# Group 0 of the sixth half batch by seven products, its mixed weights in unread quarters of w_in, and another written order

## The chip, the cores and the metric

The kernel runs on one core of one Trainium2 chip. The metric is the device time of one execution in microseconds; a kernel's time is the median of several executions. A profiled execution has a span, from its first to its last instruction, and a time of its own, a little above the span.

## What is computed

Attention over 4 batches, 8 heads, 768 tokens and 64 columns, with a band of 96 keys behind each query and 8 global keys, a bias by distance, and a softmax; then a feed-forward layer with a squared rectifier on the 3072 tokens of 512 columns:

```
scores = scale * q @ k.T + bias;  scores = where(is_global | is_local, scores, -1e9)
attn_out = softmax(scores) @ v
x = attn_out as [3072, 512]
h = maximum(x @ w_in, 0)          # w_in:  512 x 2048
out = (h * h) @ w_out             # w_out: 2048 x 512
```

The input is float32 and the kernel computes in fp16 with float32 sums.

## The kernel before

A half batch (hb 0 to 7) is 384 tokens. For each one the kernel loads q, k and v, turns q and k, forms scores, exponentials and their product with v (`score`, `attend`), turns the result into `xt` (512 columns on partitions, 384 tokens), and applies layer 1 (`w_in`) and layer 2 (`w_out`). Layer 1 of a half batch is 16 tiles of 128 hidden units, m = 0 to 15.

Layer 1 can be done in two ways. `layer1` is the plain one: for each m four matmuls of 384 columns into one bank of PSUM, then a rectification into `hr` and, for each pair of tiles, a square into `h2`. `layer1_group` takes the four tiles of a group g (m = 2g, 2g+1 and the same two 8 higher) as a 2 by 2 block product, of the two halves of w_in's rows, the near and far hidden units, and the two halves of the tokens, and computes it with seven products instead of eight (Strassen's scheme in Winograd's form). Each product is four matmuls of 192 columns. Products p1 to p7 go into two or three banks, a running sum is copied out (`keep`, tile `kept`) where it is used again, and added back (`give`). That needs sums of inputs (`x_mix`, made from `xt` by DVE) and sums of weights, four of them: for groups 1 to 3 in `in_mix`, made once at the start (`list_in_mix`); for group 0 in `late_mix` (`list_late_mix`, line 804). `GROUPS` is 1, 2, 3, and `LAYER1` says for each half batch which jobs stand in what order: a letter or digit is one product of a group (h to n is group 0), an s is a plain tile. Half batches 6 and 7 have all four groups by products; 2 to 5 have group 0 (2 also group 1) plain.

The products never read w_in's far hidden units in the first half of the rows directly. That quarter of group 0 is 2 x 256 columns on 128 partitions.

Layer 2 goes by seven products as well, for pairs of 128-token tiles (`layer2_pair`, `mix_tokens`).

Nothing orders itself: every job is first listed, TensorE's as p, loads as l, all the rest as numbers of one list, and then `Plan.run` emits them in the order of the string `ORDER`, word by word. A word is an engine's letter (p TensorE, a ACT, d DVE, s SP, l a load that POOL issues, g POOL) and the number of the job in its list; digits behind a point are the banks of PSUM that a TensorE job takes. So ORDER fixes each engine's queue, and for most jobs also the engine that does it. Each engine works its queue strictly in this order and waits where a need isn't met. The numbers shift where jobs are added to the lists: with the change TensorE has three more jobs, and the rest five more.

The loads l11, l13, l16 and l17 are w_in's quarters by hidden units, the second, first, fourth and third (512 KB each); l0, l4, l9, l12, l14, l15 are v of the first batch, l18 to l23 are k and q of the third half batch, all of 128 KB. Loads go through one queue.

Of the kernel before, what the change touches and what calls it, by code (L numbers as in the profile page):

```python
# [13 lines left out]
P = 128  # L14
# [37 lines left out]
ORDER = """a4 d1 g2 p0.0 a6 s8 d12 a0 s10 d13 l3 l1 a18 l2 d15 d19 a26 d16 d3 l5 a30 d14 a20 a27 d9 l4 a23 d5  # L52
a22 d17 p1.12+31 a21 l0 p5.34 d11 a7 p10.56 l6 a28 p3 a24 l10 a31 d32 l9 a33 p6 d34 p4.7 a39 l7
p11 d37 a29 p9.0 p8.1 a46 l8 p2.23 d43 a40 p19.7 d35 l11 a47 p7 d55 a25 p13.51 d36 l13 a41 d44
p14.4 p12.67 d48 p15 a42 l12 d59 p17 a49 p16.0 p22.2 d45 l14 p24.4 a52 d51 p23.36 a50 d38 p34.50
l16 d58 a53 p21.7 d64 p25.2 a60 l18 p27.1 d65 a57 p20.4 a61 p32.37 d66 a81 d56 p31.2 l15 p29.6 a73
d68 p18.5 p28.4 d72 a74 p26.3 l19 p36.1 d54 a69 p35.2 p30.7 a86 d70 p33.54 d85 a71 d91 p39.16 a67
p40.27 a77 p37.3 d63 l17 a82 d75 a78 d62 p41.5 a92 d79 d76 p38.0 d84 d80 l21 p45.4 d83 d96 a97 l20
p48.1 a101 a98 p44.2 l23 p47.5 a89 d107 p46.7 a112 p42.0 d111 a108 d110 a93 p43.2 d109 p53.1 a87
l22 p52.5 d102 p50.4 p49.7 d120 a113 d100 l27 a90 d105 p59.6 a116 d119 d106 a103 l29 p55.3 p51.1  # L60
d94 a122 l28 d128 a88 p65.2 d95 a104 a117 d114 p64.5 d99 a118 d146 d191 p58.4 a129 l30 a136 d115
l24 p60.0 a137 d205 l25 p54.3 p62.6 p57.1 a133 p56.7 d125 d121 p63.5 p67.6 a123 d134 d135 a130
d206 p61.1 p72.3 a126 d132 p69.7 d189 a124 p77.5 a131 d156 p70.0 a142 p82.1 d157 d165 a159 p71.4
a160 p74.7 d162 l34 a166 d201 a163 p83.6 d147 a161 l26 p73.0 d164 a167 d158 d148 a138 p84.3 l31
a168 d186 a169 p79.42 d202 l35 a139 d127 p89.01 p81.7 d151 a198 l33 p85 a187 d170 a178 d207 p86
d184 a174 a199 d149 p78.06 a179 l32 p80.45 p88.71 d180 p87 a195 d200 l36 a175 p76.2 d203 a185 d155
p75.7 l37 d193 a196 p91.0 a188 d143 l38 s194 d197 p66.1 a181 d172 l39 a171 d152 p95.3 a173 p90.4
d223 p100.2 d153 s224 a209 a176 d236 p92 d204 d177 p103.7 d208 d237 p68.3 a244 a140 d210 s216
p93.6 a211 d240 p94 a182 d150 a144 d219 p96.1 p104 s217 d225 p97 d183 a245 d221 p98.5 d239 s220
p102.3 a218 d238 p111 d214 d228 s226 l44 p106 d222 d243 l43 s229 p109.61 d213 d227 p110.53 d154  # L70
p99 l40@217 a255 d258 s215 p101 a256 d141 l42@217 d145 a251 d272 d190 p113 l45 a252 a234 p114.53
d254 l41@217 d192 p108.61 p105.0 a248 l46 d246 a261 p107 d253 d259 l47 a262 d257 s260 p115.67 a249
s235 p116.52 l48 a264 p118.3 d230 d250 p131.1 a265 d232 a268 p117.6 d263 a293 p122.7 d231 a273
d266 p121.5 a269 d233 d212 a271 p125.1 d280 s328 p124 d284 p127.2 a283 p126 d241 a278 p123.6 d267
a294 d285 p137.1 s329 d281 p119.4 a288 p132 a287 p129.5 a279 d295 p130 p140 d327 a305 p142 a286
d270 p134.6 a291 d274 a311 p128.1 a292 p135 d289 p133.7 a312 p136 d300 p141.4 a314 d303 a302
p143.1 a299 d313 s242 a296 p139 d330 s282 p138 a304 d405 p112 a309 d315 a301 l50@329 d310 s275
p120 a307 d297 a316 l56 a306 p146.36 d308 s290 p147.42 p145.51 a334 d317 l53 p144.7 a337 d322 s298
a335 l51@329 p148.3 d323 a338 a276 l52 p149.4 d325 a331 d443 d336 l49@329 a326 p151.62 a332
p150.05 d318 p152 d324 l54 a342 d333 p159.1 a343 l57 p157.0 d340 a341 p172.5 d344 a345 p153 l55  # L80
a356 d377 a346 p160.3 a354 p169.6 s378 d319 a348 p158.5 d357 p162 p161 d355 p154.2 d320 a359
p166.3 d407 a351 p164.5 p163 d360 p156 d321 a361 d363 s408 p171.1 d365 a372 p165 d347 a364 p167
a366 p181.5 d368 a369 d339 p170 a367 p175 d349 p177 d373 a362 p174.0 d382 p173.4 a386 p178.3 d380
a374 s409 p176 d376 a393 p180 d375 p155.0 a379 d353 a387 p168.1 d383 a384 d391 a394 s247 p179 d410
s277 p183 a370 s358 p182.5 d392 a352 d388 p184 l58@409 a397 d395 a385 p186.32 d389 l65 s381
p188.10 a399 p187.46 d390 a371 p185.5 l62 d398 a419 s396 p189.7 d411 a423 l59@409 a416 d412 p190.4
l63 a415 d414 a420 p191 a424 d413 l73 a417 d426 p192.13 a428 d422 l61 p193.60 a427 d421 p194.72
p196 a432 d418 l60@409 a429 d425 p198.6 a433 p195 d406 l64 a436 d401 a444 p200.1 d496 a437 p199.0
d447 a430 p202.7 d497 p218.2 s448 d445 p207.3 a475 d402 p197.1 d403 a457 s350 p206.0 d404 s446
a451 d441 p211 a442 d438 p210 a455 d435 p204.2 a462 d434 p205.7 a456 d453 p208 p213 d463 p216.0  # L90
d492 p219.2 a464 d499 d498 s507 p228.3 a454 d468 d439 a458 p209 d505 p223 a465 d476 s508 p203.4
# [113 lines left out]
def kernel(  # L205
# [18 lines left out]
    NFT = d_ff // P  # L224
# [1402 lines left out]
```

## Time and profile before

| | |
|---|---|
| median of 3 runs | 200.61 us (200.53 to 202.39) |
| the profiled execution | 200.26 us |
| its span | 198.5 us |
| TensorE's granted clock | 1.00 |
| DMA | 27.52 MB, mean 139 GB/s |

An engine's busy time is the union of its instructions. Ends of matmuls are modelled and overlap the next start, so the distance from one start to the next is what a matmul costs. PE is TensorE's matmuls, PEld its weight loads, DVE the vector engine, ACT the scalar engine, POOL GpSimd, SP the engine that issues stores and turns by DMA. In a row of a group stand line, engine, operation, output and inputs, shapes and count, then the busy time and the mean ns of one, then the idle time ahead of it and who ended it. In a row of time the first number is the start, the second the duration, in us from the span's start.

### The profile page before, as it was taken

The page shows a single profiled execution, that of the slowest core. Times are in us where ns is not written, and L with a number is a line of the kernel's source. Part 1 is how long each engine was busy: PE and PEld are TensorE (multiplying, and loading weights), DVE is VectorE, ACT ScalarE, POOL GpSimd, SP SyncE. Part 2 cuts the span into 40 slices and gives each one's busy share as a digit, 9 for nine tenths or more (in the row PEclk, how much of TensorE's full clock was granted, in tenths as well). Part 3 has the DMA queues.
Part 4 walks back from the last instruction along what each step waited for, and adds up shares of the span by engine and source line. Part 5 has one row for each costly group of instructions (what it writes and reads, how often), then busy time and mean ns, then how long its engine had stood idle before and what let it go on. Part 6 is the DMA issues. An engine that isn't in the chain of part 4 may idle for free.

```text
span 198.5 us, 5961 instructions
## 1 busy us (share of the span) xinstructions
PE 191.0 (96%) x2369; PEld 162.4 (82%) x2369; DVE 179.5 (90%) x469; ACT 159.9 (81%) x337; POOL 66.9 (34%) x82
## 2 busy tenths in 40 slices
PE   7698999999999999999999999999999999999993
PEld 2576898856998687799788988899889999999992
DVE  7689696898999989999999997999999999999971
ACT  6799896899556889989998999989797889589311
POOL 8996564187107800950293039200000000000000
PEclk9999999999999999999999999999999999999999
DMA  5999999999998999999999979994521330210124
GB/s 155 181 149 196 188 181 171 206 198 155 183 189 94 163 196 220 102 139 109 266 118 156 122 177 143 194 198 104 103 81 39 113 76 1 106 56 0 56 106 159
DMA packets 106987, 27.52 MB, mean 139 GB/s; under 512 B 97104, under 2 KB 104016, under 8 KB 106960
## 3 DMA queue, kind: packets, MB, share of 16 engines
q0 software_dynamic: 74944, 13.11, 90.5%
q1 hardware_dynamic: 30816, 13.45, 32.0%
q10 hardware_dynamic: 1200, 0.59, 1.1%
q8 instruction: 18, 0.29, 0.7%
q14 instruction: 9, 0.07, 0.1%
HBM read 27.26 MB, written 6.29 MB: 169 GB/s over the span
## 4 chain that ended last, share of the span: by engine, by line
PE 82%; DMA 10%; POOL 5%; issue 0%; DVE 0%; POOLq 0%
PE yps L1084 34%; PE hps L844 22%; PE hps L717 12%; DMA w_in_sb<-in_moe_w_in_dram 10%; PE sp L610 5%; PE av L671 4%; PE yps L998 4%; POOL w_mix L396 3%; POOL v L396 1%; PE trp L549 1%; POOL sq L396 1%; POOL sk L396 0%; PE av L1400 0%; POOL far L294 0%; DVE y L258 0%
## 5 line engine op out<-in xcount | busy, mean ns | idle before, releaser
L623 ACT ACTIVATE ex<-sp 128x512 f16<-128x512 f32 x66 | 37.6, 661 | 3.9 <-PE sp L610 3.6
L717 PE MATMUL hps<-xt,w_in_sb 128*128 128x384 f16 (+2 forms) x304 | 38.9, 275 | 0.5 <-DMA w_in_sb<-in_moe_w_in_dram 0.5
L1084 PEld LDWEIGHTS <-h 128*128 128x128 f16 x376 | 33.9, 98 | 4.5
L904 DVE TENSOR_TENSOR hr<-hps,kept 128x384 f16<-128x384 f32 x55 | 29.0, 549 | 2.0 <-PE hps L844 2.0
L717 PEld LDWEIGHTS <-w_in_sb 128*128 128x128 f16 x304 | 24.9, 98 | 7.0 <-DMA w_in_sb<-in_moe_w_in_dram 0.9
L256 ACT COPY kept<-hps 128x384 f32<-128x384 f32 x50 | 24.0, 499 | 5.5 <-PE hps L844 5.4
L1084 PEld LDWEIGHTS <-mixed 128*128 128x128 f16 x272 | 25.4, 98 | 2.7
L396 POOL DMA_DIRECT2D sq<-in_q_dram x19 | 17.2, 904 | 29.2 <-DMA q<-sq 21.3
L396 POOL DMA_DIRECT2D sk<-in_k_dram x19 | 17.1, 901 | 23.2 <-DMA q<-sq 21.4
L256 ACT COPY y<-yps 128x256 f32<-128x256 f32 (+2 forms) x38 | 14.8, 405 | 12.0 <-PE yps L1084 9.2
L844 PEld LDWEIGHTS <-in_mix 128*128 128x128 f16 x272 | 23.0, 98 | 1.3
L744 ACT ACTIVATE hr<-hps 128x384 f16<-128x384 f32 (+1 forms) x38 | 20.3, 549 | 4.5 <-PE hps L717 4.4
L844 PE MATMUL hps<-x_mix,in_mix 128*128 128x192 f16 x204 | 23.2, 246 | 0.0
L396 POOL DMA_DIRECT2D v<-in_v_dram x24 | 21.9, 925 | 1.7 <-DMA w_mix<-in_q_dram 1.0
L1084 PE MATMUL yps<-w_mix,h 128*128 128x256 f16 (+1 forms) x192 | 22.4, 264 | 0.0
L1084 PE MATMUL yps<-w_mix,mixed 128*128 128x256 f16 (+1 forms) x184 | 22.2, 268 | 0.0
L1084 PE MATMUL yps<-w_out_sb,h 128*128 128x256 f16 (+1 forms) x184 | 22.0, 268 | 0.0
L647 DVE TENSOR_TENSOR phat<-ex,mask 128x1024 f16<-128x1024 f16 (+1 forms) x36 | 20.8, 593 | 0.0
L844 PEld LDWEIGHTS <-w_in_sb 128*128 128x128 f16 x236 | 20.0, 98 | 0.9
L944 ACT ACTIVATE h<-hr 128x768 f16<-128x768 f16 x24 | 20.0, 850 | 0.4
L844 PE MATMUL hps<-xt,w_in_sb 128*128 128x192 f16 x160 | 18.8, 246 | 0.0
L758 ACT ACTIVATE h<-hr 128x768 f16<-128x768 f16 (+1 forms) x21 | 15.4, 756 | 0.2 <-DVE hr L746 0.2
(119 smaller groups left out, 370.9 us busy)
## 6 DMA issues: line engine op xcount, KB each, us to landing
out_dram<-y SPq DMA_DIRECT2D x23, 256.0 KB, 2.3
v<-in_v_dram POOLq DMA_DIRECT2D x24, 128.0 KB, 6.8
sq<-in_q_dram POOLq DMA_DIRECT2D x19, 128.0 KB, 6.4
sk<-in_k_dram POOLq DMA_DIRECT2D x19, 128.0 KB, 6.2
w_in_sb<-in_moe_w_in_dram POOLq DMA_DIRECT2D x4, 512.0 KB, 11.1
w_out_sb<-in_moe_w_out_dram POOLq DMA_DIRECT2D x4, 512.0 KB, 12.0
y<-in_k_dram ACTq DMA_DIRECT2D x2, 256.0 KB, 5.0
y<-in_q_dram SPq DMA_DIRECT2D x2, 256.0 KB, 4.4
```

The source lines that it names most:

```text
L256: nc.scalar.copy(out=out, in_=in_)
L396: dma = nc.gpsimd.dma_start(out=dst, in_=src[x.b, :, r0 + t * P:r0 + (t + 1) * P, :] .rearrange("h p d -> p h d"))
L610: nc.tensor.matmul(sp[h][:, i, :], lhsT=lhsT, rhs=x.q[rows, r % HT, a, :], start=True, stop=True)
L623: nc.scalar.activation(out=st["ex"][:, h], in_=sp[h], func=AF.Exp, scale=scale)
L647: eng(e).tensor_tensor(out=x.phat[a][:, :, t0:t0 + n], op=ALU.mult, in0=st["ex"][:, :, i0:i0 + 2 * n].rearrange("p e (t b) c -> p e t (b c ...
L717: nc.tensor.matmul(st["ps"][:, i * n:(i + 1) * n], lhsT=w_in_sb[:, kk, m * P:(m + 1) * P], rhs=x.xt[:, kk, c0:c1], start=kk == 0, stop=kk ...
L744: nc.scalar.activation(out=o, in_=i, func=AF.Relu)
L758: nc.scalar.activation(out=h2, in_=hr, func=AF.Square)
L844: nc.tensor.matmul(st[name][:, i * HC:(i + 1) * HC], lhsT=left(i, kk), rhs=right(kk), start=fresh and i == kk == 0, stop=kk == KK - 1, ski ...
L904: eng(e).tensor_tensor(out=hidden(which)[:, :, cols], in0=sums(name), in1=st[kept], op=ALU.add)
L944: nc.scalar.activation(out=h2, in_=hr, func=AF.Square)
L1084: nc.tensor.matmul(st[bank_name][:, 0:n], lhsT=a(m), rhs=b(m)[:, cols], start=fresh and m == 0, stop=m == HK - 1, skip_group_check=not fresh)
```

## The change

Group 0 of half batch 5 (the sixth) is done by seven products. Its four plain jobs go, seven jobs of four short matmuls come, with their copies, adds, rectifications and squares. The mixed weights of group 0 must then be there before the last half batch's staging of q (`y.sq`), which held three of them, is free; they move into the unread quarters of w_in, of groups 3, 2, 1 and 0. Each sum now waits for the plain products that read its quarter, and for the mixed weights of the first loading that are made from it. The weight sums are listed at the sixth half batch instead of the seventh.

```diff
-          4: "AasBbCscDEdefF123ss45gG67", 5: "1A2BCDs3E45sF6abcdefgGs7s",
+          4: "AasBbCscDEdefF123ss45gG67", 5: "1A2BCDh3E45iF6jabckdlefgGm7n",
...
-        if any(m in (NFT // 2, NFT // 2 + 1) for m in ms):
-            plain_jobs.append(job)
+        for g in {m % (NFT // 2) // 2 for m in ms if m >= NFT // 2}:
+            plain_jobs[g].append(job)
...
-    plain_jobs = []
+    plain_jobs = [[] for _ in range(4)]
...
     def list_late_mix():
-        y = halves[NHB - 1]
         near, far = slice(0, 2 * P), slice(d_ff // 2, d_ff // 2 + 2 * P)
         w = [[w_in_sb[:, a * KK:(a + 1) * KK, ms] for a in range(2)] for ms in (near, far)]
+        places = (GROUPS[2], GROUPS[1], GROUPS[0], 0)
+        late_mix.extend(w_in_sb[:, 0:KK, far.start + g * 2 * P:far.stop + g * 2 * P] for g in places)
         for i, a, b in ((0, w[1][0], w[1][1]), (1, 0, w[0][0]), (2, w[0][0], w[1][0]),
                         (3, w[0][1], 1)):
             def late_sum(e, i=i, a=a, b=b):
-                if not late_mix:
-                    rows = y.sq.rearrange("p t h d -> p (t h d)")
-                    late_mix.extend([rows[:, n * KK * 2 * P:(n + 1) * KK * 2 * P].rearrange(
-                        "p (k m) -> p k m", k=KK) for n in range(3)] + [w[1][0]])
...
-            needs = [late_mix_ops[t][0] for t in (a, b) if type(t) is int] + y.turned
-            if i == 3:
-                needs = needs + plain_jobs + late_mix_ops[2]
+            needs = [late_mix_ops[t][0] for t in (a, b) if type(t) is int] + plain_jobs[places[i]]
+            needs = needs + (late_mix_ops[0] + late_mix_ops[2] if i == 3 else
+                             in_mix_ops[0] + in_mix_ops[2])
```

ORDER is another one from its third word on. The loads around w_in, and the words around the new jobs (old ORDER first; in the new one p248, p254, p258, p262, p264, p271 and p273 are the seven products, d538 to d541 the weight sums, a550, a568, a572, d561, d574, d590, d575, d591, a594, a576 and d595 their copies, adds, rectifications and squares):

```
l3 l1 l2 l5 l4 l0 l6 l10 l9 l7 l8 l11 l13 l12 l14 l16 l18 l15 l19 l17 l21 l20 l23 l22
l1 l2 l3 l5 l4 l9 l0 l8 l7 l10 l6 l11 l13 l12 l14 l16 l17 l15 l20 l23 l22 l18 l19 l21
```
```diff
+p109.30 p99 a255 d213 d214 l40@217 a251 d258 s215 p101 d538 a256 l42@217 a252 d257 p114.56 a241
...
+d577 a559 p258.2 p269 d579 p254.3 a544 a568 s601 p262 d541 p274 d593 a572 d580 a586 d561 p271 a560
+p264 d603 p275 s578 a604 d574 a587 d590 p279 d609 a581 d575 s556 p273 d596 a620 d602 p280 a594
+a576 d591 p276.05 d595 p278.13 p277.27 a610 d624 p281.6 a617 d625 a613 p282.0 a622 d628 a611 d626
```

TensorE's jobs around the first readers of w_in's fourth quarter (p49, p51, p59) and its third (p60 and p56), in the old and the new order (the numbers are the same in both up to 247):

```
old: p53 p52 p50 p49 p59 p55 p51 p65 p64 p58 p60
new: p59 p51 p53 p49 p50 p56
```

p49, p59, p58, p60, p64 and p65 are pairs of plain tiles (eight matmuls of 256 columns), p51 and p56 four tiles (sixteen matmuls of 128 columns), p50, p52, p53 and p55 pairs of transposes.

More of the change, by code (lines that the diff above doesn't have):

```diff
@@ L50 @@
 KEEP = [0, 1, 2, 1, 6, 4, 3]
[L52 to L68, printed above, removed]
@@ L99 @@
-a535 p252 d559 a562 p253 a565 p266.4 d527 a580 p260.1 p261 d534 a581 s450 p250.5 p244 d578 a553
-a568 d548 p257 s579 a586 p259.7 d563 p264 a542 p242.4 d551 a567 s560 d554 a552 d574 p269 p263.5
-d566 a583 p248.6 d555 a540 d597 p265 a556 s596 p262 d576 p271 a546 d569 a564 p272 d598 d575 a599
-d572 p254.7 a577 d570 p276 s573 d591 a557 d571 a584 p278.3 d558 s549 d611 d600 p273.26 d635
-p274.15 d633 p275.74 a601 p277 d615 a608 a619 d616 p279.2 a609 d618 a604 p283 a602 d634 d613 a605
-p281.74 d617 s614 a631 p280.16 s593 p282.05 a624 d603 p288 a620 d587 a628 d610 p300.7 s594 p286
@@ new lines @@
+a109 l21 d100 a88 d95 p51.4 d110 a128 d112 p53.0 p49.5 d117 a113 p50.7 d191 p56.3 a116 l28 d105
+p62.2 l27 d104 d129 p52.4 l29 p57.7 d120 d119 p55.6 p60.0 d94 a122 l30 d99 a114 d125 p64.4 a118
+l24 d115 p54.6 d136 a101 p65.5 l25 d130 a123 p58.7 l26 a133 d121 d102 p69.1 d137 p61.4 p71.3 d124
+a156 p63.0 d134 p72.2 a157 d135 p70.6 d189 a132 p67.0 a138 l31 a159 d126 p76.1 a165 l34 d131 a166
+p83.4 d162 d160 a142 d201 p82.5 a158 d167 d163 p74.7 d187 a186 l36 d202 a139 p84.2 d205 a164 d169
+p89.60 d161 a127 d147 p88.34 p79.57 a198 d151 p85 a178 l35 d149 a199 p86 a195 d148 a179 p80.65
@@ L123 @@
+p379 s814 p372 d811 d810 s812 p381 a803 p382 d815 s804 s816 a817 a818"""
 class Op:
```

104 lines of the change are left out of this document (58 added, 46 removed).

## The prediction

> **What bounds the kernel now.** I read the page first, then who waited for whom on TensorE, then the busy time by stretches, then the order of time where a term needs it.
>
> ```profile
> span 198.5 us, 5961 instructions
> ...
> PE 191.0 (96%) x2369; PEld 162.4 (82%) x2369; DVE 179.5 (90%) x469; ACT 159.9 (81%) x337; POOL 66.9 (34%) x82
> ...
> PE   7698999999999999999999999999999999999993
> ...
> DVE  7689696898999989999999997999999999999971
> ACT  6799896899556889989998999989797889589311
> ```
>
> TensorE is idle only in the opening (the first four slices) and in the last slice; DVE is nearly full as well. The view of waits has for PE:
>
> ```profile
> PE sp L1350 <- ACT q L256: 0.9, 1, 0.9
> ...
> PE hps L717 <- DMA w_in_sb<-in_moe_w_in_dram: 0.5, 2, 0.3
> ```
>
> Its only wait behind 20 us is for w_in. So time is TensorE's stream from about 20 us on: work taken from it counts in full, and so does each wait that a new order brings. The stretch of the sixth half batch (hb 5, some 28 us) with the two engines that empty PSUM:
>
> ```profile
> sum 28.00, PE 28.00 PEld 24.77 DVE 27.34 ACT 25.07 POOL 1.10; mean PE 4.00 PEld 3.54 DVE 3.91 ACT 3.58 POOL 0.16
> ```
>
> The sum is over seven stretches from 124 to 152 us. PE has no gap in it, DVE 0.66 us, ACT 2.93.
>
> **The products.** Group 0 of hb 5 is now 4 plain jobs, each of 4 matmuls of 384 columns; it becomes 7 products, each of 4 matmuls of 192.
>
> ```profile
> 127.81 0.81 PE L717 MATMUL hps<-xt,w_in_sb 128*128 128x384 f16 x4
> 128.46 0.49 PE L844 MATMUL hps<-x_mix,in_mix 128*128 128x192 f16 x4
> 128.79 0.49 PE L844 MATMUL hps<-xt,in_mix 128*128 128x192 f16 x4
> 129.12 0.81 PE L717 MATMUL hps<-xt,w_in_sb 128*128 128x384 f16 x4
> 129.77 0.41 PE L844 MATMUL hps<-xt,w_in_sb 128*128 128x192 f16 x3
> ```
>
> From start to start (ends are modelled and overlap) a plain job takes 128.46 - 127.81 = 0.65 us, a product 0.33. So 7 x 0.33 = 2.31 replaces 4 x 0.65 = 2.60: -0.29 us, all of it on the path.
>
> More matmuls need more weight loads, 28 for 16:
>
> ```profile
> L844 PEld LDWEIGHTS <-in_mix 128*128 128x128 f16 x272 | 23.0, 98 | 1.3
> ```
> ```profile
> 149.93 0.68 PEld L844 LDWEIGHTS <-sq 128*128 128x128 f16 x8
> ```
>
> One lasts 98 ns, longer than the 82 ns (0.33/4) that its matmul holds the stream; but eight take 0.68, so (0.68 - 0.098)/7 = 83 ns apart: they overlap and keep up. The Trainium skill, "TensorE: Matmul & The Clock Gate", section "Back-to-back issue gap", speaks against this change: in a stream of load and matmul pairs it has about 81 ns for 128 columns and 131 for 512, so on a line between, as an estimate, 89 for 192 and 114 for 384, and 28 x 89 - 16 x 114 = +0.67 us for my -0.29. The trace disagrees: 0.65/4 = 163 ns for 384 columns, and that decides.
>
> **What empties PSUM.** Kinds and prices, from the groups between 124 and 148 us, first DVE, then ACT:
>
> ```profile
> L904 DVE TENSOR_TENSOR hr<-hps,kept 128x384 f16<-128x384 f32 x9 | 4.6, 550 | 0.0
> ...
> L946 DVE TENSOR_TENSOR h<-hr 128x768 f16<-128x768 f16 x4 | 2.1, 549 | 0.0
> ...
> L914 DVE TENSOR_SCALAR hr<-hr 128x768 f16<-128x768 f16 x3 | 1.1, 351 | 0.0
> ...
> L804 DVE TENSOR_TENSOR sq<-w_in_sb 128x512 f16<-128x512 f16 x2 | 0.8, 418 | 0.0
> ...
> L760 DVE TENSOR_TENSOR h<-hr 128x768 f16<-128x768 f16 x1 | 0.6, 551 | 0.0
> ...
> L929 DVE TENSOR_SCALAR hr<-hr 128x384 f16<-128x384 f16 x1 | 0.2, 249 | 0.0
> ```
> ```profile
> L623 ACT ACTIVATE ex<-sp 128x512 f16<-128x512 f32 x14 | 7.9, 629 | 0.8 <-PE sp L610 0.8
> L944 ACT ACTIVATE h<-hr 128x768 f16<-128x768 f16 x6 | 5.1, 850 | 0.0
> L256 ACT COPY kept<-hps 128x384 f32<-128x384 f32 x9 | 4.2, 496 | 0.1
> ...
> L744 ACT ACTIVATE hr<-hps 128x384 f16<-128x384 f32 x4 | 1.9, 486 | 0.9 <-PE hps L717 0.8
> L912 ACT ACTIVATE hr<-hps 128x384 f16<-128x384 f32 x3 | 1.6, 527 | 0.0
> ...
> L758 ACT ACTIVATE h<-hr 128x768 f16<-128x768 f16 x1 | 0.9, 856 | 0.0
> ```
>
> Removed: four rectifications of plain sums (ACT, 4 x 0.486) and two squares (0.856 ACT, 0.551 DVE). Added, by the letters in the new order: three holds (a550, a568, a572: 3 x 0.496), one rectification (a594, 0.527) and one square (a576, 0.850) on ACT; three adds (d561, d574, d590: 3 x 0.550), one late rectification over 768 (d575, 0.351), one over 384 (d591, 0.249) and one square (d595, 0.549) on DVE. Three of the four late weight sums leave this stretch, since their places no longer wait for the last half batch's turned q: d538, d539, d540 stand far ahead, among the third half batch's work (-3 x 0.418). ACT +0.07, DVE +0.99: more than DVE's 0.66 of room. But of the stretch's old operations the new order moves seven from DVE to ACT (a553, a559, a581, a583, a586, a620, a622) and three back (d593, d628, d640). At the prices above (two late rectifications and a square, 0.85 each; one over 384 columns and one of sums, about 0.5 each; two copies, about 0.4) ACT gains some 4.4 and gives 1.7, DVE loses 2.9 and gets 1.4. Then DVE has 26.8 and ACT 27.9 of a stretch of 27.7. I put the emptying at nothing, with TensorE's own work as cover; its price if that cover is gone is the slower rival.
>
> **The late sums' new waits.** The sum into place 0 (d541) waits for the fifth half batch's last plain products of group 0; the other three for the mixed weights of the first loading and plain products of half batches one to three. Behind each DVE's queue would stand still, and with it PSUM's banks. All those products stand tens of jobs ahead in the new order, so 0; a bound is one sum each, 4 x 0.418, if one came in DVE's way, and the room the moved three leave, -1.25.
>
> **The opening.** The rest of the diff is order alone, from its first words on. In the loads, l17 (w_in's third quarter) goes ahead of l18, l15 and l19, a k, a v and a k of 128 KB. Issue and landing, in order of time on POOL's queue and by the view of DMA for each:
>
> ```profile
> 14.74 0.77 POOL L454 DMA_DIRECT2D w_in_sb<-in_moe_w_in_dram  x1
> ...
> 18.51 0.88 POOL L396 DMA_DIRECT2D sk<-in_k_dram  x1
> 20.23 0.75 POOL L454 DMA_DIRECT2D w_in_sb<-in_moe_w_in_dram  x1 [0.83 <-DMA w_in_sb<-in_moe_w_in_dram]
> ```
> ```profile
> w_in_sb<-in_moe_w_in_dram POOLq DMA_DIRECT2D x1, 512.0 KB, 12.0
> ```
> ```profile
> sk<-in_k_dram POOLq DMA_DIRECT2D x1, 128.0 KB, 10.7
> ```
> ```profile
> w_in_sb<-in_moe_w_in_dram POOLq DMA_DIRECT2D x1, 512.0 KB, 12.2
> ```
>
> The fourth quarter lands at 14.74 + 12.0 = 26.74, the three small ones by 18.51 + 10.7 = 29.21, the third quarter at 20.23 + 12.2 = 32.43. Without the three (2.47 us) ahead it would land at 29.96, 2.47 sooner. But TensorE's order moves its first user too:
>
> ```profile
> 28.53 0.28 PE L1429 MATMUL trx<-ident,tm 128*128 128x128 f16 x2
> 28.64 0.28 PE L717 MATMUL hps<-xt,w_in_sb 128*128 128x128 f16 x2
> ```
> ```profile
> 32.50 0.94 PE L717 MATMUL hps<-xt,w_in_sb 128*128 128x256 f16 x7 [0.18 <-DMA w_in_sb<-in_moe_w_in_dram]
> ```
> ```profile
> 138.41 1.04 PE L1084 MATMUL yps<-w_out_sb,mixed 128*128 128x256 f16 x8
> 139.28 1.04 PE L1084 MATMUL yps<-w_mix,h 128*128 128x256 f16 x8
> ```
>
> Now that user (p60) starts at 32.50, 0.07 behind the landing. Three jobs of eight matmuls of 256 columns (p58, p64, p65; 139.28 - 138.41 = 0.87 each) and two pairs of transposes (p52, p55; 28.64 - 28.53 = 0.11 each) stand ahead of it now and behind its successor (p56) in the new order: 2.83 us. In the new order p56 can start at 29.96 + 0.07 = 30.03, with 2.83 us of old work still to do, which is as far as the old order is at 32.86: 0.36 us later than 32.50. Bounds: 0, if the quarter overtakes the small ones by more; 0.6, if it gains only two of their three slots (0.82 each) by waiting for a free place in its queue, less what TensorE can do meanwhile. I take +0.36. What lands later for it, the v and the k's, has its first users behind p56, p62 and more, and all eight transfers together are the same bytes; I cost that at nothing, and at up to 0.8 (one slot) if a turn of the third half batch comes first. The start of the layer 1 products at 20 us hangs on the eleven loads ahead of w_in's first transfer, and these are the same eleven in another order: 0.
>
> **Small gaps.** Behind 33 us the page has TensorE full, but a few weight loads start late with no releaser:
>
> ```profile
> 115.98 0.30 PEld L671 LDWEIGHTS <-phat 128*128 128x128 f16 x8 [0.16 <-issue]
> ```
>
> A new order ends this one (-0.16) and makes others. I take -0.16, from -0.4 (two or three like it) to +0.8 (four places as tight as the chain below).
>
> **The sum.** -0.29 + 0 + 0 + 0.36 - 0.16 = -0.09 us, against the profiled execution's 200.26 (span 198.5 and 1.76 around it): 200.17. The median of the runs shown is 200.61, 0.35 above that execution; with it I forecast 200.5. One per cent (2 us: below 198.6, above 202.6) is about what a measurement of this kernel can tell from no change.
>
> **Rivals.**
>
> *The copies fill ACT (slower).* ACT idles 2.93 us in the stretch now, and by the rows above at least 0.8 + 0.9 of that is waiting for TensorE at scores and sums, which another order doesn't fill. With 27.9 us of work and 1.7 of waits ACT needs 29.6 for a stretch of 27.7: TensorE waits 1.9 us for banks at the stretch's end, and where DVE, at 26.8, waits for ACT's holds in turn, up to 2.5. It decides once ACT's waits exceed 27.7 - 27.9 plus what it may lag at the end, some two operations (1.7 us). For it: the order moves 2.7 us there net. Against it: the last half batch's exponentials, a large share of ACT's work, stand at the stretch's end, and their lag can be taken behind it. Time: 202.4 + 0.2 = 202.6 to 203. Chance 0.20.
>
> *The seven products' chain shows.* Group 0 now ends the stretch: p262 leaves a sum that must be copied out (a572, 0.496, behind a568, 0.496) before p271 goes on in the same bank, and only p274 (0.87) stands between; p271 to p273 and p258 to p264 are alike. Plain jobs had no such link and filled in anywhere. At some 0.2 us short in each of four places +0.8: 201.3. Chance 0.10.
>
> *Weight loads set the pace.* If loads did not overlap, 28 x 0.098 = 2.74 against 2.60: +0.14, and 0.43 above my forecast: 200.9. The row of eight loads in 0.68 speaks against it. The skill's spacing would give 200.5 + 0.29 + 0.67 = 201.5 instead. Chance 0.03.
>
> *No wait for w_in and no gaps left (faster).* -0.29 - 0.18 (the wait at 32.50) - 0.4 = -0.87: 199.7. Past 198.6 it would need another 1.1 us from the opening, where the PE wait of 0.9 for a copied q is the only single piece of that size. Chance 0.15, a third of it past 198.6.
>
> *The change doesn't do what it says*: were w_in one object for the waits, each late sum would stop TensorE until it is written, 4 x 0.418: 202.2. One such sum is there already, and the view of its line has it 152 us in, with nobody who waited for it:
>
> ```profile
> L804 DVE TENSOR_TENSOR w_in_sb<-w_in_sb,sq x1: 416/416/416, 152.2 to 152.2; 128x512 f16<-128x512 f16 x1
> ```
>
> Chance 0.02.
>
> The forecast has the other 0.50. Range 199.4 to 202.6: below it lie about 0.08, above it about 0.12 (most of the first rival). Faster by over 1%: 0.05. Slower by over 1%: 0.17, from the first rival and a trace of the others. Within: 0.78.
>
> **What would show it.** TensorE: 16 matmuls of 384 columns fewer at L717 and 28 of 192 more at L844, starts still 82 ns apart, and no product with w_in between mixed sums waiting for DVE. At w_in's third quarter a landing near 30.0 and a wait of PE there of some 0.3 us. L804 in w_in with three sums near 60 to 85 us. The forecast falls if the view of waits has PE waiting behind 35 us for ACT or DVE by more than 0.5 us in all, if the first layer 1 product starts later than 20.2, or if ACT in the sixth half batch shows less than 1 us of idle time together with gaps on PE.

## The result, and the profile after

The changed kernel takes 202.67 us (median of 9 executions, 202.18 to 203.29); the kernel before took 200.53 us on the same chip (9 executions, 200.12 to 202.39). The ratio is 1.0097, with a 95% interval of 1.0073 to 1.012: 2.1 us slower by the medians, where 200.5 us had been forecast, and just above the range's upper end. The ratio, here and below, is worked out from the executions of both kernels, and is not quite the quotient of the two medians (1.0107 here). Executions over 1.5% above the fastest of their kernel count as slow and are left out of the medians and ratios below; of the profiled ones only that of warm_fill (a run of the second round) is such. The page of the changed kernel:

```profile
span 200.8 us, 6017 instructions
...
PE 193.1 (96%) x2381; PEld 165.0 (82%) x2381; DVE 185.9 (93%) x482; ACT 155.7 (78%) x329; POOL 67.7 (34%) x82
...
PE   7797999999999999999999999999999999999994
```

TensorE has 12 matmuls more, as summed (28 short ones for 16 long ones), and apart from the start and the end its slices are still full. Its view of waits (time in all, how often, the longest; its first line, the wait ahead of the very first matmul, is 1.2 us in both kernels):

```profile
PE trp L1261 <- DVE sk L258: 1.1, 1, 1.1
PE sp L1347 <- ACT xt L256: 0.6, 1, 0.6
PE sp L1347 <- DVE kb L258: 0.5, 1, 0.5
PE hps L717 <- DVE xt L258: 0.4, 1, 0.4
```

Three of these four waits lie ahead of the layer 1 products, the largest at the very start: the transposes of k wait for the cast of sk. The stretch of the sixth half batch, 124 to 152 us, where the copies of the seven products were to be the danger:

```profile
sum 28.00, PE 28.00 PEld 25.43 DVE 27.59 ACT 27.39 POOL 3.98; mean PE 7.00 PEld 6.36 DVE 6.90 ACT 6.85 POOL 1.00
```

ACT is filled by 2.3 us more than before and DVE by 0.25 (the row is the sum of four stretches of 7 us), and still the view of waits has no entry for PE there. The late sums (line 801 now):

```profile
L801 DVE TENSOR_TENSOR w_in_sb<-w_in_sb x4: 406/412/416, 64.8 to 140.2; 128x512 f16<-128x512 f16 x4
```

They run where they were expected, and that view names nobody who waited for them.

So the loss is not where the change computes something else. It is in the first 22 us, where only the order differs. TensorE in order of time (start, duration, line, operation, how many), after:

```profile
5.36 0.61 PE L1261 MATMUL trp<-ident,sq 128*128 128x128 f16 x4
7.11 0.61 PE L1261 MATMUL trp<-ident,sk 128*128 128x128 f16 x4 [1.14 <-DVE sk L258]
7.51 1.33 PE L1326 MATMUL sp<-early,slope_id 128*128 128x128 f16 x8
8.63 0.63 PE L1261 MATMUL trp<-ident,sq 128*128 128x128 f16 x4
9.06 0.63 PE L1261 MATMUL trp<-ident,sk 128*128 128x128 f16 x4
...
21.83 1.03 PE L717 MATMUL hps<-xt,w_in_sb 128*128 128x256 f16 x8
```

and before:

```profile
5.36 0.40 PE L1264 MATMUL trp<-ident,sq 128*128 128x128 f16 x4 [0.51 <-DVE sq L258]
5.69 0.40 PE L1264 MATMUL trp<-ident,sk 128*128 128x128 f16 x4
...
10.23 0.39 PE L1307 MATMUL trp<-ident,sq 128*128 128x128 f16 x4
10.45 0.61 PE L1329 MATMUL sp<-early,slope_id 128*128 128x128 f16 x8
...
19.99 2.81 PE L717 MATMUL hps<-xt,w_in_sb 128*128 128x128 f16 x32 [0.29 <-DMA w_in_sb<-in_moe_w_in_dram]
```

Layer 1 starts at 21.83 instead of 19.99 us. Two things are to be read here. First, an idle stretch: the transposes of sk start at 7.11 instead of 5.69 us. Second, the pace: after, four transposes take 9.06 - 8.63 = 0.43 us, 107 ns each; before, 10.45 - 10.23 = 0.22 us, 55 ns each. The same work goes at half pace. From the starts of 128-column matmuls, full pace begins at 10.65 us in this execution of the changed kernel, and at 4.2 us in that of the kernel before.

The idle stretch comes from DVE's queue. After:

```profile
4.63 0.67 DVE L258 CAST sq<-y 128x512 f16<-128x512 f32 x1 [0.69 <-DMA y<-in_q_dram]
5.22 0.76 DVE L333 TENSOR_SCALAR slope_id<-ident 128x128 f16<-128x128 f16 x3
5.53 0.66 DVE L327 CAST early<-dmask 128x384 f16<-128x384 f32 x1
6.10 0.18 DVE L333 TENSOR_SCALAR slope_id<-ident 128x128 f16<-128x128 f16 x1
6.20 0.85 DVE L258 CAST sk<-y 128x512 f16<-128x512 f32 x1
```

Before:

```profile
3.69 0.70 DVE L327 CAST early<-dmask 128x384 f16<-128x384 f32 x1
4.60 0.71 DVE L258 CAST sq<-y 128x512 f16<-128x512 f32 x1 [0.20 <-DMA y<-in_q_dram]
5.22 0.41 DVE L258 CAST sk<-y 128x512 f16<-128x512 f32 x1
```

Four slope tiles (d19, d18, d15, d22) and the 16-bit distance tile (d14) stand between the two casts now. Before, three slope tiles and the distance tile were done ahead of the cast of sq, where DVE waits for a DMA anyway, and two slope tiles were ACT's. The cast of sk starts at 6.20 instead of 5.22 us, and it takes 0.85 instead of 0.41, so it ends 1.4 us later; what made the cast itself longer is not shown.

The loads are not what holds layer 1 up. The view of w_in's tile in the changed kernel has

```profile
L454 POOL DMA_DIRECT2D w_in_sb<-in_moe_w_in_dram x4: 762/777/797, 11.3 to 15.5; - x4
...
DMA to landing us min/median/max: 8.8/11.3/13.9
```

The first transfer is issued at 11.3 us and lands 8.8 us later, at 20.1; TensorE comes for it at 21.83. In the kernel before TensorE still waited 0.29 us for it at 19.99.

Behind the start of layer 1 little is lost. To the start of the last product it is 175.77 us after and 175.06 before (+0.71), and from there to the span's end 3.21 and 3.44 (-0.23). With +1.85 for the start that makes the 2.3 us between the spans.

### The profile page after: what moved, and what is told of

It reads as the page before. It is cut to its first block, busy times and chain, and to the rows that moved or that the text cites. A ratio compares the mean times of both kernels' runs of the same rounds, so it can differ in the third digit from the quotient of the medians.

```text
span 200.8 us, 6017 instructions
## 1 busy us (share of the span) xinstructions
PE 193.1 (96%) x2381; PEld 165.0 (82%) x2381; DVE 185.9 (93%) x482; ACT 155.7 (78%) x329; POOL 67.7 (34%) x82
## 4 chain that ended last, share of the span: by engine, by line
PE 71%; DVE 17%; DMA 7%; ACT 2%; issue 1%
PE yps L1081 32%; PE hps L841 22%; PE hps L717 6%; DMA sq<-in_q_dram 5%; PE sp L610 4%; PE av L671 3%; DVE w_mix L488 2%; DVE hr L746 2%; DMA y<-in_q_dram 2%; PE yps L995 2%; DVE h L760 1%; DVE mixed L1046 1%; DVE vb L258 1%; DVE tm L1411 1%; DVE kb L258 1%
## 5 line engine op out<-in xcount | busy, mean ns | idle before, releaser
L623 ACT ACTIVATE ex<-sp 128x512 f16<-128x512 f32 x66 | 35.5, 624 | 2.4 <-PE sp L610 2.3
L717 PE MATMUL hps<-xt,w_in_sb 128*128 128x256 f16 (+2 forms) x288 | 35.4, 272 | 0.5 <-DVE xt L258 0.4
L901 DVE TENSOR_TENSOR hr<-hps,kept 128x384 f16<-128x384 f32 x58 | 30.9, 550 | 0.7 <-ACT hr L909 0.2
L256 ACT COPY kept<-hps 128x384 f32<-128x384 f32 x56 | 26.0, 487 | 5.2 <-PE hps L841 4.4
L717 PEld LDWEIGHTS <-w_in_sb 128*128 128x128 f16 x288 | 23.7, 98 | 6.8 <-issue 0.6
L256 ACT COPY y<-yps 128x256 f32<-128x256 f32 (+2 forms) x42 | 15.4, 384 | 15.4 <-PE yps L1081 13.1
L396 POOL DMA_DIRECT2D sk<-in_k_dram x19 | 18.1, 952 | 26.5 <-DMA q<-sq 21.5
L941 ACT ACTIVATE h<-hr 128x768 f16<-128x768 f16 x29 | 24.2, 847 | 1.5 <-DVE hr L911 1.3
L841 PEld LDWEIGHTS <-w_in_sb 128*128 128x128 f16 x288 | 24.3, 98 | 0.9
L744 ACT ACTIVATE hr<-hps 128x384 f16<-128x384 f32 (+1 forms) x29 | 15.3, 545 | 2.9 <-PE hps L717 2.7
L681 DVE TENSOR_TENSOR tm<-av,rec 128x384 f16<-128x384 f32 x24 | 13.4, 558 | 0.8
## 6 DMA issues: line engine op xcount, KB each, us to landing
w_in_sb<-in_moe_w_in_dram POOLq DMA_DIRECT2D x4, 512.0 KB, 11.3
```

What stands on the lines that cost most here:

```text
L256: nc.scalar.copy(out=out, in_=in_)
L396: dma = nc.gpsimd.dma_start(out=dst, in_=src[x.b, :, r0 + t * P:r0 + (t + 1) * P, :] .rearrange("h p d -> p h d"))
L623: nc.scalar.activation(out=st["ex"][:, h], in_=sp[h], func=AF.Exp, scale=scale)
L681: nc.vector.tensor_tensor(out=st["tm"].rearrange("p t e d -> p e t d"), in0=av[:, :, :, 0:D], in1=rec[:, :, :, None].to_broadcast([P, 2, H ...
L717: nc.tensor.matmul(st["ps"][:, i * n:(i + 1) * n], lhsT=w_in_sb[:, kk, m * P:(m + 1) * P], rhs=x.xt[:, kk, c0:c1], start=kk == 0, stop=kk ...
L744: nc.scalar.activation(out=o, in_=i, func=AF.Relu)
```

## The experiments

Hybrids take the words of one order up to a point and the remaining words of the other behind it, with the numbers of jobs translated. What is computed is the same in all kernels here, but for some added transposes of zeros in two runs.

**First round: which part of the order.** Theory A puts the loss into the opening, theory B into what comes behind it, the seven products with their copies and sums. Of the four kernels, old_opening and products_alone are the changed code with the old order in front (135 words, to TensorE's first layer 1 product at about 20 us; 836 words, to about 127 us), new_opening and order_alone the code before with the changed order in front (138 and 838 words):

```diff
 old_opening: changed code
-a4 d1 g2 s8 p0.0 s10 a6 d12 a0 d13 l1 l2 a21 l3 d17 d146 a29 d3 l5 a28 d9 a23 d19 d18 a26 d15 l4
+a4 d1 g2 p0.0 a6 s8 d12 a0 s10 d13 l3 l1 a18 l2 d15 d19 a26 d16 d3 l5 a30 d14 a20 a27 d9 l4 a23 d5
...
 products_alone: changed code, the old order to word 836, and in it
+p101 d538
...
+s282 d539
...
+p148 d540
```

old_opening:

> The changed kernel with the old order for its first 135 words (up to the first layer 1 product) and the new order behind them. Theory A (the new opening starts layer 1 at 21.83 us where it was 19.99, and that 1.85 us is most of the loss): 200.8 us, first layer 1 product near 20.0. Theory B (the loss lies in the seven products, their late sums or the order behind the opening): 202.5 us.

Measured: 203.55 us, ratio 1.0134 (1.0095 to 1.0173).

new_opening:

> The kernel before with the new order for its first 138 words and the old order behind them; no seven products of group 0 in the sixth half batch. Theory A: 202.4 us, first layer 1 product near 21.8. Theory B: 200.5 us, as before.

Measured: 203.11 us, ratio 1.0126 (1.0081 to 1.017).

products_alone:

> The changed kernel with the old order up to the sixth half batch (836 words, with the three early late sums put in at their new places), then the new one: the seven products without the rest of the new order. Theory A: 200.2 to 200.5 us (-0.29 for the products, some of it given back by waits of the new order's end, 0.36 us in the trace of the changed kernel at 159 and 162). Theory B with the products as the cause: over 202.

Measured: 201.87 us, ratio 1.0066 (1.0029 to 1.0103).

order_alone:

> The kernel before with the new order up to the sixth half batch (838 words, without the late sums), then the old one: the new order without the seven products. Theory A: 203.0 us (+1.85 from the opening, some +0.7 from waits between 33 and 140 us that the old order hasn't). Theory B with the products as the cause: 200.5.

Measured: 204.27 us, ratio 1.0165 (1.0134 to 1.0196). The kernel before had 200.91 us beside all four.

As times these fit neither theory well, because a hybrid pays at its seam. The view of waits of old_opening has

```profile
PE hps L716 <- DMA w_in_sb<-in_moe_w_in_dram: 1.9, 1, 1.9
```

at 30 us: the old sequence of loads met TensorE's new order, which reads w_in's third quarter sooner. In products_alone and order_alone four or five waits, 1.7 and 2.4 us in all, stand between 125 and 134 us, where the orders are glued together. What can be read from them is the start of layer 1: 20.37 and 19.75 us with the old opening, 22.16 and 21.65 with the new one, whichever code runs. That is theory A's, and the question became what it is in the opening.

**Second round: the cast, and the pace.** casts_first takes the changed kernel and moves five of DVE's words back:

```diff
-l3 d17 d146 a29 d3 l5 a28 d9 a23 d19 d18 a26 d15 l4
-d14 d22 a24 d5 a20 p1.12+31 l9 d11 d16 p10.34 d7
+l3 d17 d146 a29 d3 d19 d18 d15 d14 l5 a28 d9 d5 a23 a26 l4
+d22 a24 a20 p1.12+31 l9 d11 d16 p10.34 d7
```

> The changed kernel with VectorE's opening words moved back to the old sequence: the three slope tiles and the 16-bit distance tile ahead of the cast of sq, the cast of sk right behind it; all other words as changed. Theory A (the late cast of sk leaves TensorE idle from 5.66 to 7.10 us, and that idle stretch keeps its products at half pace, 106 ns for 128 columns, until 10.6 us): no idle stretch, half pace until 7.2 us at the latest, layer 1 starts at 20.0 to 20.5, 201.0 to 201.4 us. Theory B (the late start comes from the other moved words of the opening: slopes, copies, loads): the idle stretch goes but layer 1 still starts at 21.3 or later, 202.2 or more.

Measured: 201.25 us, ratio 1.0012 (0.9983 to 1.0041). Layer 1 starts at 20.46 us. With five words moved the kernel is 0.5 us above the kernel before of its round (200.73), where the changed one is 2.1 above; theory B's 202.2 is out.

late_cast makes the mirror image in the kernel before:

```diff
-l2 d15 d19 a26 d16 d3 l5 a30 d14 a20 a27 d9 l4 a23 d5
+l2 a26 d3 l5 a30 a20 a27 d9 d15 d19 d16 d14 l4 a23 d5
```

> The kernel before, with one move: VectorE's three slope tiles and its 16-bit distance tile go between the cast of sq and the cast of sk. Theory A: TensorE idles over 1 us between the transposes of sq and of sk, its products stay at half pace until about 10 us or fall back to it, layer 1 starts at 21.3 to 22.0 instead of 20.0, 201.9 to 202.6 us. Theory B: the idle time that the kernel before has at 7.1 and 7.9 us (1.5 us in all) takes up the delay, layer 1 starts by 20.6, 200.6 to 201.1 us.

Measured: 201.1 us, ratio 1.0036 (1.001 to 1.0062), so by the median theory B; but the profiled execution took 202.04 us, with layer 1 starting at 22.14 us, which is theory A, and so did two more of the twelve take over 202 us. The two can only be reconciled by more than one profiled execution (below). The mirror is not exact either: the cast of sk takes 0.41 us here, and TensorE waits 0.6 us for it, where it waits 1.1 in the changed kernel.

warm_fill adds work where TensorE idles:

```diff
                     if i == 0:
                         warm(st[0].rearrange("p j a c -> p (j a c)"))
+                    else:
+                        for _ in range(14):
+                            nc.tensor.transpose(out=st[1][:, 0, 0, :], in_=zero[:, 0:P], identity=ident)
```

> The changed kernel with 14 transposes of zeros added between the transposes of sq and of sk, into the half bank that sk's then overwrite; VectorE's order as changed, so sk comes just as late. Theory A: TensorE is busy through the wait, full pace (56 ns) comes by 7.5 us, layer 1 starts at 20.0 to 20.8, 201.0 to 201.7 us, though sk is no earlier. Theory B: the start hangs on the late inputs, layer 1 starts at 21.6 to 22.0, 202.5 to 202.9 us.

Measured: 202.91 us, ratio 1.0102 (1.0059 to 1.0145), a miss for theory A. Its profiled execution says little, since the first q tile landed at 5.3 us there and the idle stretch stood ahead of the added transposes.

products_old is the changed code with the old order to the end, and the seven products in the region of the four plain ones:

> The changed code in the old order from the first word to the last: the four plain products of group 0 in the sixth half batch give their places to the seven, the late sums stand where the changed order has them. So the products and the sums alone, with no seam between two orders. Theory A (the opening lost the time, the products gain their 0.29 us): 200.2 to 200.6 us, layer 1 starts at 19.7 to 20.4. Rival C (the seven products, their copies or the early sums cost time themselves): 201.0 us or more with the same start of layer 1, and new waits between 125 and 145 us or behind the sums.

Measured: 203.87 us, ratio 1.015 (1.0107 to 1.0192), by its time and its new waits what rival C had said. Layer 1 starts at 19.56 us as expected, but to the last product it is 178.17 us. Its view of waits has, among others,

```profile
PE hps L840 <- ACT kept L255: 0.9, 1, 0.9
PE hps L840 <- DVE hr L900: 0.3, 1, 0.3
```

and its waits and gaps between 127 and 147 us make 3.0 us, the largest of them a product waiting for a sum that is to be copied out of its bank (`kept`, 0.9). This is the chain that the prediction's second rival spoke of. An order that was not made for the seven products pays for it; so this run prices that placing of them, and not the products.

**Third round: cleaner cuts.** At 366 words of the old order and 368 of the new one, at about 33 us, the same jobs but two are done in both. old_until is the changed code with the old order to there, new_until the code before with the new one:

> The changed code with the old order for its first 366 words (to about 33 us, where both orders have the same loads and the same steps behind them but one), then the changed order to the end. Theory A (the opening lost 1.8 of the 2.1 us; the products gain 0.29, small waits of the new order behind it cost about 1): layer 1 starts at 19.6 to 20.4, from there to the last product 175.5 to 176.2 us, 200.8 to 201.4 us. If the time stays above 202, the loss sits behind 33 us.

Measured: 201.84 us, ratio 1.0048 (1.0027 to 1.0069), layer 1 from 19.98 us. The start is back, and the time is below 202, though above theory A's 201.4; 1.6 us of new waits at 61 to 71 us (176.66 us to the last product) hide the rest of the gain.

> The kernel before with the changed order for its first 368 words (the same cut), then the old order to the end: the new opening alone, no products, no late sums. Theory A: layer 1 starts at 21.5 to 22.2, from there to the last product 174.8 to 175.5 us, 202.0 to 202.6 us. Theory D (the loss sits in the order behind 33 us): 200.5 to 201.0 us.

Measured: 203.21 us, ratio 1.0111 (1.008 to 1.0141). The new opening alone, without any product or sum of the change, costs by the median what the whole change costs. The profiled execution, though, took 201.81 us, with layer 1 from 20.43 us, and one of the other seven 201.09.

plain_new is the code before in the changed order, plain products and late sums put back:

> The kernel before in the changed order from the first word to the last: the four plain products back in the places where the seven begin, the late sums back at the end of the order beside their old neighbours. Theory A (the seven products and the sums are worth about what was summed, a gain of 0.29 us): 202.8 to 203.2 us, from the start of layer 1 to the last product 175.9 to 176.4 us. Rival C (products, copies or sums cost time): below 202.4 us.

Measured: 204.79 us, ratio 1.0171 (1.0138 to 1.0204): above both theories. TensorE waits 1.1 us for a copied y at 140 us and 0.5 us for a late sum at 155 us; once more a price of placing.

warm_fill once more, as warm_fill_2:

> The changed kernel with 14 transposes of zeros between those of sq and of sk, a second look, as the first one's profiled execution had its first q tile land 0.7 us later than the others (5.3 instead of 4.6 us) and so an idle stretch ahead of the added transposes. Theory A (the clock): where the tile lands by 4.7 us TensorE has no idle stretch over 0.7 us before 7.5 us, full pace comes by 7.5 us and stays, layer 1 starts by 20.8. Theory B (late inputs): layer 1 starts at 21.6 to 22.5 although full pace comes by 7.5 us.

Measured: 202.6 us, ratio 1.0092 (1.006 to 1.0124). Here the q tile landed in time:

```profile
5.75 1.62 PE L1260 MATMUL trp<-ident,early 128*128 128x128 f16 x14
7.21 0.39 PE L1263 MATMUL trp<-ident,sk 128*128 128x128 f16 x4
...
21.03 1.76 PE L716 MATMUL hps<-xt,w_in_sb 128*128 128x256 f16 x21
```

The idle stretch is gone, full pace comes at 7.2 us, and layer 1 starts at 21.03 us though sk comes as late as in the changed kernel: between the two theories, 0.8 us sooner than 21.83, but 0.2 past theory A's bound. So both pace and late inputs have a share. As a remedy the filling is worth nothing: the median stays where it was. The profiled execution's span is 199.6 us, and its time 2.5 us more, where the profiled executions of the other kernels lie 1.8 to 2.0 us above their spans; why is not shown.

**Fourth round: the same kernel twice.** The moment at which full pace begins is not the kernel's alone, so a second execution of the same kernel can separate it from the order of the inputs.

> The kernel before with the slope tiles and the distance tile between the casts of sq and sk, a second look. In the first look half pace lasted to 14.0 us and layer 1 started at 22.1 us (202.0 us); most of its timed runs were at 200.9 to 201.1. Theory A: if this execution is at 201.1 or less, full pace comes by 7.5 us and stays, and layer 1 starts at 20.0 to 20.9 with the idle stretch still there. Theory B: the start is late (21.3 or more) again.

Measured: 200.68 us, beside 200.73 for the kernel before. The two executions of late_cast, the first:

```profile
6.56 0.61 PE L1262 MATMUL trp<-ident,sk 128*128 128x128 f16 x4 [0.60 <-DVE sk L256]
6.96 1.91 PE L1327 MATMUL sp<-early,slope_id 128*128 128x128 f16 x16
8.67 0.63 PE L1262 MATMUL trp<-ident,sq 128*128 128x128 f16 x4
...
22.14 0.68 PE L715 MATMUL hps<-xt,w_in_sb 128*128 128x128 f16 x9
```

and the second:

```profile
6.56 0.40 PE L1262 MATMUL trp<-ident,sk 128*128 128x128 f16 x4 [0.81 <-DVE sk L256]
6.80 1.20 PE L1327 MATMUL sp<-early,slope_id 128*128 128x128 f16 x16
7.83 0.39 PE L1262 MATMUL trp<-ident,sq 128*128 128x128 f16 x4
...
20.05 2.81 PE L715 MATMUL hps<-xt,w_in_sb 128*128 128x128 f16 x32
```

sk's transposes start at 6.56 us in both. The sixteen products behind them take 8.67 - 6.96 = 1.71 us in one and 7.83 - 6.80 = 1.03 in the other; half pace goes on to 14.0 us in the first, and layer 1 starts 2.1 us apart. With the inputs as late in both, it is the pace.

> The kernel before with the changed order for its first 368 words, a second look. In the first look TensorE was at full pace by 5.4 us and stayed there through the idle stretch, and layer 1 started at 20.4 us (201.8 us); six of its eight timed runs were at 202.9 to 203.6. Theory A (pace): if this execution is one of those, it shows half pace for 3.4 us between 7 and 12 us and layer 1 starting at 21.7 to 22.2, with the same idle stretch and the same steps. Theory B (late inputs): full pace as in the first look, and the later start comes from a longer idle stretch or other waits ahead of layer 1.

Measured: 201.35 us, and again an execution at full pace, this time from 5.5 us:

```profile
7.10 0.40 PE L1262 MATMUL trp<-ident,sk 128*128 128x128 f16 x4 [1.28 <-DVE sk L256]
7.33 0.22 PE L1327 MATMUL sp<-early,slope_id 128*128 128x128 f16 x1
7.90 0.56 PE L1327 MATMUL sp<-early,slope_id 128*128 128x128 f16 x7 [0.35 <-DVE slope_id L331]
...
20.58 2.25 PE L715 MATMUL hps<-xt,w_in_sb 128*128 128x256 f16 x27
```

The idle stretch is no shorter than in the changed kernel, and layer 1 starts at 20.58 us. That gives, from one execution, what the late cast and the other moved words cost at full pace: 20.58 - 19.99 = 0.6 us, where the changed kernel loses 1.85.

> The changed kernel unchanged, a second look. Theory A: whatever moment full pace begins, half pace takes at least 3.4 us of TensorE's time behind 5 us, once or in two stretches, and layer 1 starts at 21.4 to 22.2. Theory B: layer 1 starts at 21.8 also with full pace from 7.5 us on.

Measured: 202.28 us; half pace to 10.6 us, layer 1 from 21.65 us.

casts_slopes goes one step beyond casts_first, with two slope tiles for which TensorE had waited there:

```diff
-d9 d5 a23 a26 l4 d22 a24 a20 p1.12+31 l9 d11 d16 p10.34 d7
+d9 d5 d22 d16 a23 a26 l4 a24 a20 p1.12+31 l9 d11 p10.34 d7
```

> The changed kernel with VectorE's opening as in casts_first and the slope tiles d22 and d16 also ahead of the second pair of casts, for which TensorE waited 1.1 us at 5.9 us in casts_first. Theory A: no idle stretch over 0.8 us before 8 us, layer 1 starts at 19.8 to 20.4, 200.7 to 201.2 us, level with the kernel before; no gain on it, since 175.7 us follow instead of 175.1. If it stays at 201.3 or more, the wait for the slopes cost nothing.

Measured: 201.08 us, ratio 1.0011 (0.9985 to 1.0037):

```profile
5.35 0.61 PE L1260 MATMUL trp<-ident,sq 128*128 128x128 f16 x4
5.75 0.63 PE L1260 MATMUL trp<-ident,sk 128*128 128x128 f16 x4
...
20.32 2.47 PE L716 MATMUL hps<-xt,w_in_sb 128*128 128x256 f16 x29
```

No idle stretch, and the loss is gone: seven of DVE's words carry 1.8 of the 2.1 us (2.14 above the kernel before with them as changed, 0.35 above it with them back). The products, the sums and all other words of the changed order are in this kernel.

Last, plain_casts: casts_slopes with the four plain products of group 0 in places of the seven, the late sums left early.

> As casts_slopes (the changed order with the opening's casts and slopes back), but group 0 of the sixth half batch by its four plain products, in places of the seven, and the late sums left where the change has them (the last of the four behind the last plain product): so the seven products undone and nothing else. If the products are worth the summed 0.29 us: from the start of layer 1 to the last product 175.9 us (175.6 with the seven), 201.3 to 201.5 us. If their copies and adds cost time: 175.4 or less, below 201.0. If 176.4 or more, the order, made for seven products, has waits of its own around the four, and the run can't price them.

Measured: 201.6 us beside 200.89 for the kernel before; ratio 1.0006 (0.9974 to 1.0039). By the medians it stands 0.71 us above the kernel before, and casts_slopes 0.35; that difference is about the size of the summed gain, but the ratios (1.0006 and 1.0011) rank the two the other way, and their intervals cover each other. The profiled execution was the longest of 13 (202.62 us), with waits of its own and 177.36 us from the start of layer 1 to the last product, so by the expectation the run cannot price the products. Their own gain is not shown, and a cost of theirs is not shown either.

What all the profiled executions say together, by the order of time of each; the third column is the start of layer 1, the fourth from there to the start of the last product, the last the time of that execution (us):

| kernel | half pace until | layer 1 | to the last | time |
|---|---|---|---|---|
| before | 4.2 | 19.99 | 175.06 | 200.26 |
| products_old | 5.8 | 19.56 | 178.17 | 202.98 |
| products_alone | 6.1 | 19.75 | 176.94 | 201.72 |
| old_until | 5.5 | 19.98 | 176.66 | 201.66 |
| late_cast_2 | 5.4 or sooner | 20.05 | 175.39 | 200.68 |
| plain_casts | 6.3 | 20.27 | 177.36 | 202.62 |
| casts_slopes | 7.2 | 20.32 | 175.58 | 200.99 |
| old_opening | 5.7 to 6.2 | 20.37 | 177.50 | 203.12 |
| new_until | 5.4 or sooner | 20.43 | 176.12 | 201.81 |
| casts_first | 4.0 | 20.46 | 175.67 | 201.20 |
| new_until_2 | 5.5 | 20.58 | 175.52 | 201.35 |
| warm_fill_2 | 7.2 | 21.03 | 175.34 | 202.11 |
| order_alone | 10.65 | 21.65 | 177.84 | 204.71 |
| after_2 | 10.6 | 21.65 | 175.55 | 202.28 |
| plain_new | 4.8, again 8.2 to 11.6 | 21.65 | 178.05 | 204.69 |
| after | 10.65 | 21.83 | 175.77 | 202.67 |
| late_cast | 14.0 | 22.14 | 174.68 | 202.04 |
| new_opening | 5.4 or sooner, again 8.6 to 12.0 | 22.16 | 175.27 | 202.64 |
| warm_fill | 10.3 | 22.49 | 176.16 | 204.91 |

Wherever half pace ended by 7.2 us and did not come back, layer 1 started by 21.03 us; wherever it held or came back beyond, at 21.65 or later.

## Why the forecast was wrong

**The step that failed** is the opening: "The start of the layer 1 products at 20 us hangs on the eleven loads ahead of w_in's first transfer, and these are the same eleven in another order: 0." The loads did not decide it: w_in's first transfer landed at 20.1 us. TensorE's own work ahead of layer 1 did, once a reordered DVE queue let it wait for 1.1 us between sq and sk and its half pace lasted to 10.65 us: +1.85 us in the profiled execution. With seven of DVE's words moved back (casts_slopes) layer 1 started at 20.32 us and 1.8 of the 2.1 us were gone. The prediction had listed every moved load and read TensorE's moved steps, but of DVE's moved words it read none ahead of 20 us, though the diff showed d5 behind d19, d18, d15, d14 and d22. It also rested on one execution, in which full pace began at 4.2 us, and had no case in which the pace itself changes. The prediction's own sign was right: it "falls ... if the first layer 1 product starts later than 20.2".

How the 1.85 us divide is an estimate from single executions: 0.6 for the late inputs and the other moved words at full pace (new_until_2), and so 1.2 or so for the pace; late_cast's two executions show that pace alone can be worth 2.1. The idle stretch does not cost the pace every time: new_until has the opening of the changed kernel, and three of its nine executions took 201.81 us or less, while none of the changed kernel's ten took less than 202.18.

**The third quarter of w_in**, +0.36: not met. The quarter, the last of the four transfers in the view above, landed at 15.5 + 13.9 = 29.4 us, about 0.5 sooner than worked out, and the view of waits behind 30 us has no DMA left (0.2 before). That is not only because TensorE was 1.85 us late: in casts_slopes, where layer 1 starts at 20.32 us, the view has no wait for w_in either. In its place stands, in the changed kernel, the 0.4 us wait for a copied xt.

**Small gaps**, -0.16: mis-sized. Behind the start of layer 1 the changed kernel takes 0.71 us more, with 0.29 fewer in the products by the sum, which leaves +1.0 for new gaps and waits where -0.16 was taken and +0.8 was the upper bound. That is one pair of executions. The table has 175.3 to 175.8 us there for five executions with the changed kernel's words from there on (after, after_2, casts_first, casts_slopes, warm_fill_2) and 174.7 to 175.4 for three with the old ones (before and late_cast's two), so by their means some +0.5, and +0.8 for the gaps.

**The products**, -0.29: the counts came out as summed (12 matmuls more), and the paragraph on small gaps takes the term as it was. A kernel that isolates it could not be had without new waits, so its size stays argued from the trace.

**Emptying PSUM and the late sums' waits**, 0 and 0: right. ACT went to 27.39 us of 28 (27.9 of 27.7 had been worked out), DVE to 27.59 (26.8 worked out), and PE still has no wait for either listed in that stretch. The slower rival (202.6 to 203) had the sign and the size of the result by coincidence, for its place was another; the chain of the seven products shows only in orders not made for them (products_old), and TensorE did not wait for a late sum in the changed kernel (in plain_new it did, for 0.5 us). Weight loads set no pace: two neighbouring products of 192 columns still start 82 ns apart there (median of 118), as in these rows of the changed kernel's order of time, (133.59 - 133.26)/4:

```profile
133.26 0.49 PE L841 MATMUL hps<-x_mix,w_in_sb 128*128 128x192 f16 x4
133.59 0.49 PE L841 MATMUL hps<-x_mix,in_mix 128*128 128x192 f16 x4
```

## What to carry to other kernels

Where an order is replaced as a whole, read the first microseconds of every engine's queue word by word, and not only the loads: a cast that moves behind five small steps can decide when a matrix engine is busy enough to reach full pace. Take the pace at the start (ns between two equal matmuls) from more than one execution before it goes into a sum, for one execution may have been lucky in it. And a hybrid of two orders prices its own seam; undo a handful of words instead, and profile a kernel twice when its profiled execution and its median disagree.

## What the hardware did that was not expected

TensorE's pace in the opening has its own steps, of 3.4 us. In new_opening it was at full pace from 5.4 us, idled, and lost it again; the view by stretches (busy time of PE, PEld, DVE, ACT, POOL, then the granted clock) has

```profile
4.20:8.60 4.40, 2.65 (x29) 1.77 (x28) 3.62 (x10) 1.62 (x5) 4.40 (x5) 1.00 1.96 209
8.60:12.00 3.40, 3.40 (x41) 3.01 (x39) 1.71 (x3) 2.52 (x6) 3.40 (x5) 0.50 3.10 150
12.00:14.00 2.00, 2.00 (x41) 1.79 (x40) 1.70 (x6) 2.00 (x5) 1.95 (x4) 1.00 2.88 146
```

The clock is 0.50 for one piece of 3.4 us and 1.00 around it. In the changed kernel the half pace from 7.2 to 10.6 us has another row:

```profile
7.20:10.60 3.40, 3.31 (x31) 3.05 (x32) 1.79 (x5) 1.30 (x3) 3.40 (x5) 1.00 2.49 154
```

Matmuls start 107 ns apart there, and the granted clock reads 1.00: the pace that a kernel begins with does not show in that row, only a loss of pace does. The mean clocks of the timed executions fit this: six of the changed kernel's nine show 0.989 to 0.992 (a loss of half the pace for 3.4 of 201 us would be 1 - 1.7/201 = 0.992), the other three 1.00, and all nine took 202.18 us or more; of casts_slopes' twelve none is below 0.998. So, by these clocks, the changed kernel paid for the idle stretch either way: full pace came late, or it was taken away.

The Trainium skill, "TensorE: Matmul & The Clock Gate", section "What's actually happening", describes a clock that starts at half rate and is set by how busy TensorE was in a window of about 3.4 us that runs freely, not from a kernel's start. The pieces of 3.4 us and the moments that differ from one execution to the next agree with it. The section "Why this matters for your kernels" of the same page of the Trainium skill names idle gaps of some 3 us as what loses the rate. Here less was enough: in new_opening two pieces of 1.35 and 0.35 us, with TensorE busy for 2.65 of the 4.4 us ahead of the loss, while new_until_2 kept its pace through two such pieces (1.28 and 0.35, busy for 2.74). Where exactly the limit lies was not settled.
